# A seven-product MoE kernel: order of the sums' tiles, place of the rounding, operands copied from x

## The chip, the cores and the metric

One core of a Trainium2 chip. The metric is the device time of one execution in microseconds (us). Most executions of a kernel agree within 0.3%.

## The reference, cut to what matters

```python
x = attention(q, k, v)            # k and v averaged over 8 neighbours; 4 batches, 8 heads, 576 tokens, 64 wide
x = x.reshape(2304, 512)          # N tokens, D
p = domain_probs / (domain_probs.sum(-1, keepdims=True) + 1e-09)
for e in range(4):                # moe_w1 [4, 512, 1024], moe_w2 [4, 1024, 512]
    h = np.maximum(x @ w1[e], 0)
    y += p[:, e:e+1] * (h @ w2[e])
a, b = y @ g_w1, y @ g_w2         # [512, 1024] each, float64 inputs
out = (a * b @ g_w3) @ g_wout     # [1024, 1024], [1024, 512]
```

## The kernel before, in words

**Number form.** Each matrix product is made of three matmuls: every operand is held as a high and a low part in fp32r (`hi_lo`, L175: ScalarE, short ACT, copies the high part at L176, another engine subtracts at L177), and `mm3` (L170 to 173) adds high x low, low x high and high x high in one PSUM bank.

**Stages.** A lead of some 25 us brings in q, k, v and makes the first block of x. Then expert 0 runs over 6 blocks of 384 tokens, with 8 units per block (`run_units`; one unit is the hidden rows `expert_h` and, two units later, their second products). Between the halves of the units, `between(n)` runs the pieces of attention for later blocks that lie in the list `hooks[n]`, and the loop after it those in `also[n]`; n counts half units, about 2.1 us each. `accumulate` (L667) multiplies by the weight p at L671 and stores a block of the result `acc_d` at L672.

Experts 1 to 3 run over 4 batches of 576 tokens each (`batch`, L1123), twelve in all. A batch first makes the hidden rows, in 4 calls of `hidden(j)`, each a `seven` (L882): seven products of half-size blocks (Strassen's way in Winograd's form) in place of eight. The operand holds for each half kc of the depth 7 parts in high and low: B11, B21, B22, which are quarters of x itself, and T1 to T4, sums of quarters. VectorE (DVE) adds the products up at L888: `u`, `v`, then the pair `c1` (lower sums), `u` again, then the pair `c0` (upper sums). `c0` and `c1` come from one ring of three tiles, in the order in which they are asked for. `sink` finishes a pair: ReLU on ScalarE at L1114, the high part at L176, the low part on GpSimd (POOL) at L177. The sink of `c1` runs inside its seven, that of `c0` after the first product of the next seven (`settle`). PSUM has eight banks that the products take in turn.

Then come the second products, two half-batches g of 8 steps, 12 matmuls each, into four banks. At the end of a half, VectorE multiplies by p (L1179, four times) and GpSimd adds to `acc` (L1180). In steps 0 to 7, eight DMAs (`fetch_operand`, L792) bring the next batch's operand. In an expert's last batch, `weights_of(j)` (from L718) makes the next expert's seven weight blocks and their sums; the sums `s` (L733 to 736) have one tile for all j. All DMAs are issued on SP's queue in program order.

**The rounding.** The float64 weights of the last stages come as two 32-bit words and are rounded by VectorE and GpSimd in 80 steps (`Rounding.step`, L260): seven or eight operations on VectorE (L271 to L278, for g_w3 a transposition at L309), one on GpSimd (L279), a load (L251), and a store of the step before (L297, L312 four times, or L700). `load` keeps two loads in flight. Before the change a middle batch does 3 steps in its sevens (after seven 1, 2 and 3), 3 in steps 1, 3, 5 of the second products and 2 in steps 9 and 11.

**Operands.** While expert 0's blocks 2 and 3 run, GpSimd adds the parts of x (`keep_x`, L527, in hooks from 35 on) and SP stores the sum to DRAM (`x_d`). From half unit 53 on, `load_x` (L746) loads it batch by batch, `prepare_x` (L827) makes the four sums (L834 to 837) and splits all seven parts, and `keep_operand` stores the whole operand of a batch to DRAM in quarters. Meanwhile `at_pairs` places `weights_of` 0, 1, 2 of expert 1 at units 36, 38, 41.

**w2.** For expert 1 it is split at the end of expert 0. For experts 2 and 3, eight splits lie in the sevens of the expert's first batch, one on VectorE and one on GpSimd per seven.

**The start.** `fetch` issues loads in the order of use when a staging place is free; during the lead only those in `soon`. q tiles from the fourth on come as `qb` in small packets (L447) and are transposed by VectorE (`make_qT`, L462).

Of the kernel before, what the change touches and what calls it, by code (L numbers as in the profile page):

```python
# [17 lines left out]
def fused_kernel(  # L18
# [93 lines left out]
    def packed(base, sizes, most):  # L112
        rings, at = {}, 0
# [25 lines left out]
    p_area = area("p", HT, F32, "pb")  # L139
    ap1, ap2 = area("ap1", 4 * XO, F32, "ap1"), area("ap2", 3328, F32, "ap2")  # L140
    acc_a = Places(acc=row(plain, 0, XT, 2))
    xfpool = Places(xf=row(plain, 2 * XT, HT, 4))
# [92 lines left out]
    class Rounding:  # L235
# [8 lines left out]
        def load(self):  # L244
            while self.todo and len(self.loaded) < 2:
# [74 lines left out]
    with tc.manual_schedule():  # L320
# [9 lines left out]
            **packed(ap2, [("kb", NCH * 2 * D * 4, 1), ("pT", P * 4, 1)], 3328))  # L330
# [194 lines left out]
        x_d = dpool.tile([P, KC, NT], F32, tag="x", name="x")  # L525
# [86 lines left out]
        hooks[3] = kT1[:1]  # L612
        hooks[4] = kT1[1:] + do_qT(TPB + 1)
# [14 lines left out]
        for n, i in enumerate((1, 2, 0, 3, 4, 5)):  # L628
            for hp in range(NP):
                hooks[35 + 4 * n + hp].append((None, lambda i=i, hp=hp: keep_x(i, hp)))  # L630
# [126 lines left out]
        wop_home = [2, 3, 4, 0]  # L757
# [24 lines left out]
        def part_of(b, kc, n):  # L782
            step = 2 * XO // 4 // PIECES
            cols = slice(n * step, (n + 1) * step)
            return whole(kc)[:, cols], kept_x[b][kc].rearrange("p n a s -> p (n a s)")[:, cols]

        def keep_operand(b, kc, ns=range(PIECES)):
            for n in ns:
                here, there = part_of(b, kc, n)
                nc.sync.dma_start(there, here)  # L790

        def fetch_operand(b, kc, n):  # L792
            here, there = part_of(b, kc, n)
            nc.sync.dma_start(here, there)
            xo_next[kc] = x_places[kc]

        def enter_preps():
            late["small"] = Places(xr=Ring(area("x0h", XT, F32, "xr"), [0]), t=Ring(area("x0l", XT, F32, "t"), [0]))
# [555 lines left out]
```

## Time and profile before

| | |
|---|---|
| runs | 1264.73, 1264.85, 1265.68 us (median 1264.85) |
| profiled execution | 1264.25 us |
| its span, first to last instruction | 1262.5 us |
| TensorE matmuls busy | 95% of the span |
| VectorE, GpSimd, ScalarE busy | 69%, 41%, 30% |
| DMA moved | 230.1 MB, mean 182 GB/s |

PE is TensorE (PEld its weight load), DVE is VectorE, ACT is ScalarE, POOL is GpSimd, SPq is SP's queue, which issues the DMAs. L171 is line 171 of the kernel before. "out<-in" names the tiles written and read. PEclk is the granted TensorE clock as a share of full speed, 2.4 GHz; 0.5 is 1.2 GHz. A matmul's busy time overlaps the next one's, so a full PE is not a PE at its peak.

### The profile page before, as it was taken

Reading aid. Unit: us, or ns where it says so; the run is one execution under the profiler, and the core shown is the slowest. Engines: PE = TensorE matmul, PEld = TensorE weight load, DVE = VectorE, ACT = ScalarE, POOL = GpSimd, SP = SyncE. Lnnn points to the kernel's source line nnn. Section 1 sums busy time; section 2 is a strip of 40 time slices with the busy share of each in tenths; the row PEclk is TensorE's granted clock in tenths of the full one; section 3 lists DMA queues with packets and bytes.
Section 4 is the critical chain, followed back from the end, with each engine's and each line's share of the span. In section 5 each row is a group of like instructions: output and inputs, shape, how many; then the busy total and the mean of one; then the engine's idle time right before and its main releaser. Section 6 shows DMA issues by size and latency. Waiting matters only on the chain.

```text
span 1262.5 us, 21704 instructions
## 1 busy us (share of the span) xinstructions
PE 1194.8 (95%) x7965; PEld 1142.5 (90%) x7965; DVE 871.3 (69%) x1855; ACT 373.1 (30%) x687; POOL 516.9 (41%) x569
## 2 busy tenths in 40 slices
PE   7899999989999999789999989999999999999998
PEld 6799999889999989789999979999977999999998
DVE  7677545575777777667677777777759777785554
ACT  4433333344131224313122341220336233241010
POOL 6765441133444346535434654454420222252112
PEclk9899999999999999999999989999999999999999
DMA  8757335786645663564766255656467155665541
GB/s 196 181 135 163 119 105 205 250 293 223 230 165 201 176 207 97 160 195 129 230 193 213 83 176 199 204 198 206 160 191 266 44 203 192 238 232 199 214 175 42
DMA packets 182191, 230.10 MB, mean 182 GB/s; under 512 B 52860, under 2 KB 121540, under 8 KB 182084
## 3 DMA queue, kind: packets, MB, share of 16 engines
q1 hardware_dynamic: 182084, 228.72, 56.6%
q8 instruction: 62, 1.02, 0.3%
q14 instruction: 45, 0.37, 0.1%
HBM read 152.08 MB, written 76.58 MB: 181 GB/s over the span
## 4 chain that ended last, share of the span: by engine, by line
PE 48%; DVE 15%; POOL 12%; DMA 11%; issue 7%; ACT 4%; SPq 2%; POOLq 0%; DVEq 0%; ACTq 0%
PE g L171 9%; PE g L172 9%; PE g L173 9%; POOL round L177 6%; PE s L171 6%; PE s L173 6%; PE s L172 6%; DVE plain L888 4%; ACT plain L1114 2%; POOL x5l L279 2%; POOL plain L1180 2%; DMA w<-x5l 2%; ACT round L176 2%; DMA x5h<-in_moe_w_dram 2%; PE sc L475 1%
## 5 line engine op out<-in xcount | busy, mean ns | idle before, releaser
L177 POOL TENSOR_TENSOR round<-plain,round 128x576 fp32r<-128x576 f32 x128 | 185.9, 1454 | 357.5 <-ACT round L176 301.5
L171 PE MATMUL g<-round,w2h 128*128 128x288 f32 (+1 forms) x960 | 299.3, 312 | 27.6 <-DVE plain L888 20.2
L172 PE MATMUL g<-round,w2l 128*128 128x288 f32 (+1 forms) x960 | 294.1, 306 | 0.0
L173 PE MATMUL g<-round,w2h 128*128 128x288 f32 (+1 forms) x960 | 294.0, 306 | 0.0
L171 PE MATMUL s<-xo,wh 128*128 128x288 f32 x840 | 252.9, 301 | 14.1 <-DVE plain L888 8.5
L173 PE MATMUL s<-xo,wh 128*128 128x288 f32 x840 | 250.7, 298 | 0.0
L172 PE MATMUL s<-xo,wl 128*128 128x288 f32 x840 | 250.4, 298 | 0.0
L171 PEld LDWEIGHTS g<-round,w2h 128*128 128x128 f32 x960 | 183.9, 192 | 34.7 <-DVE plain L888 23.0
L172 PEld LDWEIGHTS g<-round,w2l 128*128 128x128 f32 x960 | 184.0, 192 | 0.0
L173 PEld LDWEIGHTS g<-round,w2h 128*128 128x128 f32 x960 | 183.5, 191 | 0.0
L171 PEld LDWEIGHTS s<-xo,wh 128*128 128x128 f32 x840 | 160.5, 191 | 17.4 <-DVE plain L888 9.5
L888 DVE TENSOR_TENSOR plain<-s,plain 128x288 f32<-128x288 f32 x320 | 133.4, 451 | 42.6 <-PE s L173 25.2
L172 PEld LDWEIGHTS s<-xo,wl 128*128 128x128 f32 x840 | 160.5, 191 | 0.2
L173 PEld LDWEIGHTS s<-xo,wh 128*128 128x128 f32 x840 | 160.6, 191 | 0.0
L176 ACT ACTIVATE round<-plain 128x576 fp32r<-128x576 f32 x132 | 89.7, 682 | 162.0 <-DVE plain L1207 159.0
L279 POOL TENSOR_TENSOR x5l<-x5l 128x256 f32<-128x256 f32 x80 | 58.7, 734 | 180.4 <-DVE x5l L278 180.4
L1114 ACT ACTIVATE plain<-plain 128x576 f32<-128x576 f32 x96 | 65.3, 680 | 218.7 <-DVE plain L888 218.7
L888 DVE TENSOR_TENSOR plain<-s,x5h 128x288 f32<-128x288 f32 x160 | 67.2, 454 | 65.1 <-POOL round L177 54.4
L890 ACT ACTIVATE plain<-s 128x288 f32<-128x288 f32 x80 | 31.7, 396 | 230.8 <-PE s L173 230.8
L171 PE MATMUL g<-xl,round 128*128 128x384 f32 x192 | 67.4, 351 | 4.6 <-DVE round L656 4.6
L656 DVE SCALAR_TENSOR_TENSOR round<-g,round 128x384 fp32r<-128x384 f32 x48 | 26.4, 552 | 61.6 <-ACT round L655 61.5
L173 PE MATMUL g<-xh,round 128*128 128x384 f32 x192 | 65.3, 340 | 0.0
(238 smaller groups left out, 2275.6 us busy)
## 6 DMA issues: line engine op xcount, KB each, us to landing
xo<-keptx SPq DMA_DIRECT2D x72, 504.0 KB
raw<-in_moe_w_dram SPq DMA_DIRECT2D x64, 256.0 KB
x5h<-in_moe_w_dram SPq DMA_DIRECT2D x64, 256.0 KB
keptx<-xo SPq DMA_DIRECT2D x32, 504.0 KB
plain<-acc SPq DMA_DIRECT2D x12, 1152.0 KB
acc<-plain SPq DMA_DIRECT2D x12, 1152.0 KB
kept<-xo SPq DMA_DIRECT2D x12, 576.0 KB
xo<-kept SPq DMA_DIRECT2D x10, 576.0 KB
```

The costliest lines, as they stand in the source:

```text
L171: nc.tensor.matmul(ps, lh, rl, start=first, stop=False)
L172: nc.tensor.matmul(ps, ll, rh, start=False, stop=False)
L173: nc.tensor.matmul(ps, lh, rh, start=False, stop=last)
L176: nc.scalar.activation(hi, src, AF.Copy)
L177: (lo_eng or nc.vector).tensor_tensor(lo, src, hi.bitcast(F32), op=ALU.subtract)
L279: nc.gpsimd.tensor_tensor(a, a, b, op=ALU.add)
L475: nc.tensor.matmul(sc[off:off + n, (hp % 2) * W:(hp % 2 + 1) * W], qT[:, hp, off:off + n], kT_t[b][:, hp * W:(hp + 1) * W], start=True, st ...
L656: nc.vector.scalar_tensor_tensor(hl, ps, 0.0, hh.bitcast(F32), op0=ALU.max, op1=ALU.subtract)
L888: nc.vector.tensor_tensor(to, one, two, op=ALU.add)
L890: nc.scalar.activation(x, product(j, A11, B11), AF.Copy)
L1114: nc.scalar.activation(r, r, AF.Relu)
L1180: nc.gpsimd.tensor_tensor(acc[:, d, cols], acc[:, d, cols], part, op=ALU.add)
```

## The change

1. `seven` asks for `c1` before `c0`, and takes a function `meanwhile` that it calls after the second product's addition.
2. The rounding keeps three loads in flight (three places). A middle batch does one step in its sevens, in seven 2 (an expert's last batch, but not the very last, two, in sevens 1 and 2), and seven in the second products, at steps 1, 3, 5, 7, 9, 10, 12.
3. `acc` and `pb` are loaded after seven 1 instead of ahead of the batch.
4. w2 is streamed in the order of use (`turn_of`). Five of its eight splits move to VectorE, in steps 11 to 15 of the last batch before; three stay in the first batch's sevens, on GpSimd.
5. The operand's B parts are copied by DMA from the high and low parts of x into the DRAM tile `kept_x[b]`. GpSimd adds the parts of x in SBUF for the sums; only the sums are split, and stored by `keep_sums`. The first batch's B parts are fetched back by `fetch_parts`.
6. The batches go 2, 3, 0, 1, then 1, 0, 3, 2, then 2, 3, 0, 1 (before 0 to 3, 3 to 0, 0 to 3). `at_pairs` is 38, 41, 46; blocks of x are freed and reused in another order (`wop_home`).
7. In the lead the second `qb` is in `soon`, and its transposition moves from hook 4 to hook 3.
8. Areas: one `acc` tile in expert 0 instead of two; `ap2` is merged into `p_area`.

```diff
-    acc_a = Places(acc=row(plain, 0, XT, 2))
-    xfpool = Places(xf=row(plain, 2 * XT, HT, 4))
+    acc_a = Places(acc=Ring(plain, [0]))
...
-            while self.todo and len(self.loaded) < 2:
+            while self.todo and len(self.loaded) < 3:
...
-        def keep_x(i, hp):
-            xh, xl = x_t[i]
-            xf = xfpool.tile([P, BLK], F32, tag="xf")
-            nc.gpsimd.tensor_tensor(xf, xh[:, hp].bitcast(F32), xl[:, hp].bitcast(F32), op=ALU.add)
-            nc.sync.dma_start(x_d[:, hp, i * BLK:(i + 1) * BLK], xf)
+        kept_x = [dpool.tile([P, 2, 2, 7, HB], F32, tag=f"keptx{b}", name="keptx") for b in range(B)]
+        def keep_x(i, m):
+            src = x_t[i][m].bitcast(F32)
+            done = 0
+            while done < BLK:
+                b, at = divmod(i * BLK + done, S)
+                a, at = divmod(at, HB)
+                n = min(BLK - done, HB - at)
+                part = src[:, :, done:done + n]
+                if a == 0:
+                    for half in range(2):
+                        nc.sync.dma_start(kept_x[b][:, :, m, half, at:at + n], part[:, 2 * half:2 * half + 2])
+                else:
+                    nc.sync.dma_start(kept_x[b][:, :, m, 2, at:at + n], part[:, 2:])
+                done += n
...
-        hooks[3] = kT1[:1]
-        hooks[4] = kT1[1:] + do_qT(TPB + 1)
+        hooks[3] = kT1[:1] + do_qT(TPB + 1)
+        hooks[4] = kT1[1:]
...
-        wop_home = [2, 3, 4, 0]
+        wop_home = [0, 2, 3, 4]
...
+        def keep_sums(b, kc, ms=range(2)):
+            sums = whole(kc).rearrange("p (n a s) -> p n a s", n=2, s=HB)
+            for m in ms:
+                nc.sync.dma_start(kept_x[b][:, kc, m, 3:], sums[:, m, 3:])
+        def fetch_parts(b, kc):
+            there = whole(kc).rearrange("p (n a s) -> p n a s", n=2, s=HB)
+            for m in range(2):
+                nc.sync.dma_start(there[:, m, :3], kept_x[b][:, kc, m, :3])
+            xo_next[kc] = x_places[kc]
+        def rows_of_x(b, kc):
+            r = late["small"].tile([P, 2, 2, HB], F32, tag="xr")
+            flat = r.rearrange("p n a s -> p n (a s)")
+            done = 0
+            while done < S:
+                i, at = divmod(b * S + done, BLK)
+                n = min(S - done, BLK - at)
+                hi, lo = (t.bitcast(F32).rearrange("p (n k) s -> p k n s", k=2)[:, kc, :, at:at + n] for t in x_t[i])
+                nc.gpsimd.tensor_tensor(flat[:, :, done:done + n], hi, lo, op=ALU.add)
+                done += n
+            sums_t[kc] = None, r
+        def sums_of_x(kc):
+            _, r = sums_t[kc]
+            t = late["small"].tile([P, 4, HB], F32, tag="t")
...
+        def split_sums(kc):
+            (_, th), (_, tl) = x_places[kc]
+            hi_lo(th, tl, sums_t.pop(kc)[0])
...
-        def seven(j, sink):
+        def seven(j, sink, meanwhile=None):
-            c0, c1 = (late["small"].tile([P, 2, HB], F32, tag="c", name=t, bufs=3) for t in ("c0", "c1"))
+            c1, c0 = (late["small"].tile([P, 2, HB], F32, tag="c", name=t, bufs=3) for t in ("c1", "c0"))
...
             add(u, product(j, S2, T2), x)
+            if meanwhile:
+                meanwhile()
             add(v, product(j, S3, T3), u)
...
+        for n, (b, kc) in enumerate((b, kc) for b in order for kc in range(2)):
             begin = 2 * FIRST + 5 * n
+            at_place(begin - 1, lambda b=b, kc=kc: rows_of_x(b, kc))
+            at_place(begin, lambda kc=kc: sums_of_x(kc))
+            at_place(begin + 1, lambda kc=kc: split_sums(kc))
+            for m in range(2) if b != order[-1] else ():
+                at_place(begin + 2 + m, lambda b=b, kc=kc, m=m: keep_sums(b, kc, [m]))
+            if b == order[-1]:
+                at_place(begin, lambda b=b, kc=kc: fetch_parts(b, kc))
+        at_pairs = {38: 0, 41: 1, 46: 2}
...
-        soon = [("qb", TPB)] + [("k", 1, c) for c in range(NCH)]
+        soon = [("qb", TPB)] + [("k", 1, c) for c in range(NCH)] + [("qb", TPB + 1)]
...
-            acc = small.tile([P, KC, S], F32, tag="acc")
-            nc.sync.dma_start(acc, acc_d[:, :, b * S:(b + 1) * S])
-            pb = load_pb(e, b)
             for j in range(NJ):
-                hidden(j)
+                some = j == 2 or last and not end and j == 1
+                hidden(j, (lambda: round_some(1)) if some else None)
...
-                if n == 0 and e > 1:
-                    stream.split(nc.vector)
+                if n == 0 and e > 1 and j < FC - AHEAD:
                     stream.split()
...
-                if j and not (last and j == 3):
-                    round_some(1)
+                if j == 1:
+                    acc = small.tile([P, KC, S], F32, tag="acc")
+                    nc.sync.dma_start(acc, acc_d[:, :, b * S:(b + 1) * S])
+                    pb = load_pb(e, b)
...
                     elif last:
                         if step in (1, 4, 7, 10):
                             weights_of((step - 1) // 3)
+                        if step >= 2 * FC - AHEAD:
+                            stream.split(nc.vector)
...
-                    if step in (1, 3, 5) and (end or not last) or step in (9, 11) and not last:
+                    if step in (1, 3, 5, 7) and (end or not last) or step in (9, 10, 12) and not last:
                         round_some(1)
...
-        orders = {e: list(range(B))[::1 if e % 2 else -1] for e in range(1, E)}
+        orders = {1: [2, 3, 0, 1], 2: [1, 0, 3, 2], 3: [2, 3, 0, 1]}
```

`order` is [0, 1, 3, 2] and AHEAD is 5. `step = g * 8 + k` counts the steps of the second products; `last` is an expert's last batch, `end` the very last.

## Rows read from the trace of the kernel before

**Rows 1.** Page, part 1: engine, busy us (share of the span) xinstructions

```profile
PE 1194.8 (95%) x7965; PEld 1142.5 (90%) x7965; DVE 871.3 (69%) x1855; ACT 373.1 (30%) x687; POOL 516.9 (41%) x569
```

**Rows 2.** Stages: start:end width, PE, PEld, DVE, ACT, POOL busy (x), PEclk, DMA, GB/s

```profile
0.00:50.00 50.00, 37.47 (x217) 31.86 (x218) 34.47 (x59) 19.76 (x40) 34.89 (x67) 0.94 0.77 188
...
192.47:294.33 101.86, 93.55 (x519) 92.59 (x517) 59.44 (x107) 36.25 (x64) 21.74 (x17) 0.97 0.68 233
...
294.33:928.83 634.50, 596.48 (x4322) 587.10 (x4321) 464.18 (x1093) 174.30 (x302) 307.20 (x296) 0.98 0.57 182
```

**Rows 3.** Same view, single stretches: a hidden stage, second products, expert 0

```profile
349.09:371.43 22.34, 22.34 (x170) 22.34 (x169) 16.56 (x42) 8.80 (x16) 11.27 (x11) 1.00 0.52 173
...
529.73:562.47 32.74, 27.68 (x195) 27.08 (x193) 23.47 (x56) 4.70 (x8) 14.63 (x15) 0.95 0.58 168
...
200.00:225.00 25.00, 25.00 (x146) 25.00 (x145) 14.91 (x27) 7.93 (x13) 0.00 (x0) 1.00 0.58 213
```

**Rows 4.** Waits of PE, 294.33 to 928.83: us in total, times, longest us

```profile
PE g L171 <- DVE plain L888: 20.2, 12, 3.8
...
PE s L171 <- DVE plain L888: 8.5, 3, 3.0
...
PE s L171 <- DMA xo<-keptx: 3.3, 4, 1.8
```

**Rows 5.** Groups of DVE, 294.33 to 928.83: busy us, mean ns, idle before <-releaser

```profile
L888 DVE TENSOR_TENSOR plain<-s,x5h 128x288 f32<-128x288 f32 x96 | 39.5, 453 | 56.2 <-POOL round L177 51.6 <-PE s L173 1.8 <-DMA acc<-plain 1.6
...
L1179 DVE TENSOR_TENSOR s<-g,ap 128x288 f32<-128x288 f32 x46 | 20.9, 454 | 26.5 <-POOL plain L1180 26.3 <-PE g L173 0.2
...
L177 DVE TENSOR_TENSOR w2l<-raw,w2h 128x512 fp32r<-128x512 f32 x8 | 12.8, 1598 | 7.7 <-ACT w2h L176 7.7
...
L177 DVE TENSOR_TENSOR round<-raw,round 128x512 fp32r<-128x512 f32 x7 | 4.9, 707 | 5.7 <-ACT round L176 5.7
```

**Rows 6.** Timeline of DVE: start us, us, line, operation [idle before <-releaser]

```profile
375.43 0.82 DVE L888 TENSOR_TENSOR plain<-s,x5h 128x288 f32<-128x288 f32 x2 [1.30 <-POOL round L177]
...
377.66 0.29 DVE L273 TENSOR_SCALAR x5l<-x5l 128x256 f32<-128x256 f32 x1
...
377.99 1.49 DVE L275 TENSOR_SCALAR x5l<-x5l 128x256 uint32<-128x256 uint32 x1
...
437.53 0.29 DVE L271 TENSOR_SCALAR x5l<-x5h 128x256 uint32<-128x256 uint32 x1 [2.54 <-DMA x5h<-in_moe_w_dram]
...
442.14 0.30 DVE L271 TENSOR_SCALAR x5l<-x5h 128x256 uint32<-128x256 uint32 x1 [2.14 <-DMA x5h<-in_moe_w_dram]
...
444.54 0.45 DVE L1179 TENSOR_TENSOR s<-g,ap 128x288 f32<-128x288 f32 x1
```

**Rows 7.** Waits of SP's queue: us in total, times, longest us

```profile
SPq L1127 <- DMA acc<-plain: 53.3, 12, 5.9
```

**Rows 8.** Timeline of DVE, end of the last batch of expert 1

```profile
502.23 1.01 DVE L177 TENSOR_TENSOR wl<-raw,wh 128x512 fp32r<-128x512 f32 x2
```

**Rows 9.** Groups of instructions, whole span, POOL and ACT

```profile
L177 POOL TENSOR_TENSOR round<-plain,round 128x576 fp32r<-128x576 f32 x128 | 185.9, 1454 | 357.5 <-ACT round L176 301.5
...
L1114 ACT ACTIVATE plain<-plain 128x576 f32<-128x576 f32 x96 | 65.3, 680 | 218.7 <-DVE plain L888 218.7
...
L530 POOL TENSOR_TENSOR plain<-xh,xl 128x384 f32<-128x384 f32 x24 | 23.5, 1008 | 6.9 <-DVE xl L177 6.9
```

**Rows 10.** Groups of DVE, 192.47 to 294.33

```profile
L834 DVE TENSOR_TENSOR t<-xr 128x288 f32<-128x288 f32 x8 | 3.6, 453 | 8.4 <-DMA xr<-x 8.4
```

**Rows 11.** Waits of PE, first 50 us, then 192.47 to 294.33

```profile
PE sc L475 <- DVE ap L462: 4.5, 1, 4.5
...
PE g L171 <- DVE round L656: 4.6, 2, 2.9
...
PE g L171 <- DVE plain L671: 3.7, 1, 3.7
```

**Rows 12.** Timeline of SP's queue: start us, us, line, DMA xcount

```profile
36.70 4.36 SPq L447 DMA_DIRECT2D stxl<-in_q_dram  x8
```

More of the change, by code (lines that the diff above doesn't have):

```diff
@@ L110, in row, with packed @@
         return Ring(base, [at + size * n for n in range(bufs)])
-    def packed(base, sizes, most):
-        rings, at = {}, 0
+    def packed(base, sizes, most, begin=0):
+        rings, at = {}, begin
         for tag, size, bufs in sizes:
@@ L627, in fused_kernel @@
             hooks[10 * i + 4][:0] = do_attend(i)
-        for n, i in enumerate((1, 2, 0, 3, 4, 5)):
-            for hp in range(NP):
-                hooks[35 + 4 * n + hp].append((None, lambda i=i, hp=hp: keep_x(i, hp)))
+        for i in range(NB):
+            for m in range(2):
+                hooks[35 + 4 * i + 2 * m].append((None, lambda i=i, m=m: keep_x(i, m)))
         for b, at_v, at_k, at_kT in ((1, 3, None, None), (2, 15, 15, 20), (3, 26, 25, 30)):
@@ L780, in fused_kernel, with fetch_operand @@
         PIECES = 4
-        def part_of(b, kc, n):
+        def fetch_operand(b, kc, n):
             step = 2 * XO // 4 // PIECES
             cols = slice(n * step, (n + 1) * step)
[L785 to L794, printed above, removed]
-            xo_next[kc] = x_places[kc]
+            nc.sync.dma_start(whole(kc)[:, cols], kept_x[b][:, kc].rearrange("p n a s -> p (n a s)")[:, cols])
+            xo_next[kc] = x_places[kc]
@@ new lines, in keep_sums @@
+        def keep_sums(b, kc, ms=range(2)):
[4 more added lines that the diff above has]
+            there = whole(kc).rearrange("p (n a s) -> p n a s", n=2, s=HB)
+            for m in range(2):
+                nc.sync.dma_start(there[:, m, :3], kept_x[b][:, kc, m, :3])
[11 more added lines that the diff above has]
+            sums_t[kc] = None, r
@@ L797, in enter_preps @@
         def enter_preps():
[L798 removed]
+            late["small"] = Places(xr=Ring(plain, [2 * XT]), t=Ring(plain, [XT]))
         def enter_weights():
@@ L936, in rows, with at_place @@
             return w3_blocks[u[1][0]][1] if u[0] == "w" else TPB
-        kept_x = [[dpool.tile([P, 2, 7, HB], F32, tag=f"keptx{b}{kc}", name="keptx") for kc in range(2)] for b in range(B)]
         x_places = []
-        preps = [(b, kc) for b in (1, 2, 3, 0) for kc in range(2)]
+        order = [0, 1, 3, 2]
         FIRST = ATT_BLOCKS * FC + 4
         also = {}
-        for n, (b, kc) in enumerate(preps):
-            begin = 2 * FIRST + 5 * n
-            also.setdefault(begin - 3, []).append(lambda b=b, kc=kc: load_x(x_d, b, kc))
-            for m in range(3):
-                also.setdefault(begin + m, []).append(lambda b=b, kc=kc, m=m: prepare_x(kc, x_places[kc], n=m))
-            for m in range(PIECES if b else 0):
-                also.setdefault(begin + 3 + m, []).append(lambda b=b, kc=kc, m=m: keep_operand(b, kc, [m]))
-        also[2 * FIRST - 3].insert(0, enter_preps)
-        also[2 * FIRST].insert(0, enter_late)
-        at_pairs = {36: 0, 38: 1, 41: 2}
-        also.setdefault(2 * 36, []).append(enter_weights)
+        def at_place(n, f):
+            also.setdefault(n, []).append(f)
+        at_place(2 * FIRST - 1, enter_preps)
+        at_place(2 * FIRST, enter_late)
+        for n, (b, kc) in enumerate((b, kc) for b in order for kc in range(2)):
+            begin = 2 * FIRST + 5 * n
+            at_place(begin - 1, lambda b=b, kc=kc: rows_of_x(b, kc))
[6 more added lines that the diff above has]
+        at_pairs = {38: 0, 41: 1, 46: 2}
+        also.setdefault(2 * 38, []).append(enter_weights)
         for n, j in at_pairs.items():
@@ L1107, in load_pb, with hidden @@
             return pb
-        def hidden(j):
+        def hidden(j, meanwhile=None):
             def sink(n, c, other):
@@ L1115, in sink @@
                 hi_lo(t[:, 0], t[:, 1], r, nc.gpsimd)
-            seven(j, sink)
+            seven(j, sink, meanwhile)
         def round_some(n):
@@ L1146, in batch @@
                     add_pair(e + 1, j)
-                for fc in range(FC):
+                for fc in turn_of:
                     add_w2(e + 1, fc)
```

24 lines of the change are left out of this document (15 added, 9 removed).

## Prediction

> **What bounds the kernel now.** The profiled execution took 1264.25 us, 0.60 under the median of the runs (1264.85); its span is 1262.5, so 1.75 lie around it. The sum below is made on the profiled execution. I read the page's busy times first [rows 1]: TensorE's matmuls fill 95% of the span, VectorE 69%. So only time that TensorE loses can be won, and the shares don't say where it is lost. The busy times by stage do [rows 2], held against undisturbed stretches [rows 3]. A hidden stage is 28 products of 6 matmuls; its 168 (the row counts two neighbours) took 22.34 us, 0.133 each. The twelve batches, 4320 such matmuls (row: 4322), would take 574.5 and take 634.5: **60.0 lost**. The stage 192 to 294 holds 516 matmuls of 384 columns (row: 519); at 25/144 = 0.174 (row: 146, two at the edges) they take 89.6 and took 101.9: **12.3 lost**. The first 50 us have 12.5 idle and a granted clock of 0.94, 3.0 more. The code of what follows 929 is not touched.
>
> Next, who ends TensorE's waits [rows 4]. In the batches it is VectorE's additions at L888, 20.2 + 8.5 = 28.7 in 15 waits; the clock took a good part of the rest. The second-product stretch from 529.73 shows the pair: 5.1 idle, and 0.95 of the clock over 32.7 us, 1.6 more [rows 3].
>
> Why is VectorE late? A seven is 42 matmuls, 5.6 us. VectorE's seven additions take 7 x 0.45 = 3.2 [rows 5]. The third, the first into the tile of the lower sums, waits about 1.3 for GpSimd [rows 6]: 51.6 in all [rows 5]. That tile is the previous seven's upper one, whose rounding ends late. Then comes one rounding step: 2.4 alone (442.14 to 444.54), 3.5 beside GpSimd, when one operation of 0.25 to 0.3 takes 1.49 [rows 6]. 3.2 + 1.3 + 3.5 = 8.0 against 5.6, three times per batch: VectorE ends the sevens some 6 us behind. TensorE can run eight PSUM banks ahead, no further, and so the second products begin with a wait.
>
> **Part by part.**
>
> *Lower sums take their tile first.* With three tiles, the lower sums of seven j now get the tile of the upper sums of j-2, the upper ones that of the lower of j-1. The new pair is 5.6 us apart or more; its chain (two activations of 0.68, GpSimd's 1.45 [rows 9]) takes 2.8. I take the whole wait as gone. If it stayed, a seven without rounding would still be 4.5 against 5.6, so this edit alone decides little.
>
> *Rounding.* A middle batch keeps 8 steps: 1 in a seven (3.2 + 3.5 = 6.7, 1.1 behind, made good in the next), 7 in the second products. The third product of the third seven must be taken when TensorE comes to its bank again, 6.4 us after writing; the step leaves 2.9 spare. In the second products VectorE has 3.5 + 3 x 2.4 = 10.7 of steps in the first half (12.8 long), 3.0 of multiplications (four of 0.45, and 26.5/23 = 1.2 of waits for GpSimd [rows 5]), then 3.3 + 2 x 2.4 = 8.1: 21.8 of the 25.5 us that 192 matmuls take. Loads are the open point: 437.53 to 442.14 a step came every 4.6 us, held 2.1 by its load [rows 6]. Three loads in flight instead of two should bring it near 2.9, since a load then has two steps to land; ends 2.4 and 4.6. On SP's queue each step issues a load and a store (four where it transposes); behind them stand the next operand's eight transfers. Those waited for a late VectorE before and start earlier now.
>
> *acc and pb loads after the second seven.* SP stood 53.3 us in 12 waits before them for the store of the batch before [rows 7]. There now only steps with 10 us to spare stand behind them; acc is first used 24 us later. Cost 0; without that cover a late acc would hold GpSimd's addition.
>
> *w2.* At two changes of expert, eight splits stood in the sevens; four on VectorE took 1.60 each [rows 5]. Now three stay, on GpSimd (3 x 1.45 = 4.4 of 5.6), and five go to VectorE in the last half-batch, behind four weights_of that hang on one tile of sums. The fourth's VectorE part ended at 503.24, 28.2 after the stretch began at 475.05 [rows 8]; about 5 of that was the lag. So 23 + 5 x 1.6 = 31, and the next batch needs the first bank of that half at 25.5 + 3.2 = 28.7: 2.3 wait, 1.6 of clock, **about 4 each**, 0 (0.71 each, as w_out's splits [rows 5]) to 9 (five waits for loads). The slow row is w2l at 1.60 beside GpSimd. The Trainium skill ("SBUF — State Buffer", Who interferes with whom) has a VectorE instruction with two SBUF inputs wait for the whole of a GpSimd one that reads SBUF, which speaks against this move; by it, each behind a whole operation of 1.45, the five would take 5 x (0.71 + 1.45) = 10.8 instead of 8.0, 5.6 us more over both changes.
>
> Batches together, losses left: the first 2 (weights_of stays in its sevens, and the first load of the rounding has nothing ahead of it), two changes 8, four batches of transposed steps 1 each, others about 0.2: 15 of 60.0. **Gain 45**; 25 to 56.
>
> *x.* Before, GpSimd adds x (24 x 1.01 [rows 9]), SP stores it and loads it 16 times. VectorE waited 8.4 for that in this stage [rows 10], SP being behind block stores, and TensorE waited 4.6 + 3.7 for VectorE [rows 11]. After: 36 copies of 98 to 295 KB straight from x in an earlier stretch, the 24 stores of operand quarters here become 12 of 590 KB (and the eight in the first batch four), the first batch's operand is completed by four loads, and GpSimd adds eight times 1152 columns, 8 x 3.0, in a stage where it was busy 21.7 of 102 [rows 2]. It runs ahead by its own semaphores, so no wait; cover gone, up to 3 per operand. VectorE also drops the splits of the B parts. Left: at the second weights_of, now beside the same block's multiplications, about 2 with 1.6 of clock. **Gain 8.5**; 3 to 12.
>
> *Start.* TensorE waited 4.5 at 39.8 for VectorE's transposition of the second q tile [rows 11], whose eight transfers went out at 36.70 [rows 12]. They now go out right behind the first k loads, for the same 4.4 us of SP; behind them stand the last k chunk and w2 loads. Gain 4.5 + 3.0 of clock, less about 1.5: **6**; -1 (they delay the start's loads by their 4.4) to 8.
>
> *At nothing:* order of batches, homes of weights, merged areas, one acc tile instead of two (stores 35 us apart), at_pairs later by 2 to 5 units (the sevens need them later still), the order of w2. If at_pairs came late, the first batch's sevens would wait.
>
> Sum: 45 + 8.5 + 6 = 59.5; 1264.25 - 59.5 = 1204.75, **1205 us**; own range 1193 to 1220.
>
> **Rivals.** (a) *Operands late.* Four steps now share the first half with 4.0 MB of operands. For: TensorE did wait for these (3.3 in four [rows 4]). Against: they start once the sevens have read the old ones, and no longer when a lagging VectorE lets SP go on. Price: nine changes of batch within an expert x (2.0, a little over the longest such wait, + 1.6 of clock) = 32: 1237.
> (b) *Slower: loads set the pace of seven steps.* If steps come 4.6 apart as at 437, VectorE has 0.5 + 7 x 4.6 + 3.0 = 35.7 us before the last multiplications, the first of which frees its bank at 36.2 where TensorE wants it at 28.7; nine batches lose 7.5 + 1.6 = 9.1: 1205 + 82 = 1287. It starts to cost at a step of 3.5 and eats all the gain at 4.3. For: those rows [rows 6]. Against: they are two deep, and the step itself is 2.4.
> (c) *TensorE isn't held by the lag*, only by banks and chains that stay: the batches keep their 60, 1264.25 - 14.5 = 1250. Against: sevens whose VectorE is on time (349.09) lose nothing.
> (d) *It doesn't do what it says*: new waits for GpSimd's additions and SP's copies eat all: 1264.
>
> **Numbers.** Chances: forecast 0.66, (a) 0.15, (b) 0.07, (c) 0.06, (d) 0.06, half of it on either side. Range 1193 to 1238: forecast and (a); left out are (b), (c), (d). A measurement of this kernel can tell 0.2% (2.5 us) from no change. Faster 0.66 + 0.15 + 0.06 + 0.02 = 0.89, same 0.03, slower 0.07 + 0.01 = 0.08.
>
> **What would show it.** L888 no longer waits for GpSimd's rounding; TensorE's waits for L888 fall from 28.7 to under 8; a middle batch takes 48 us; no VectorE wait for xr; no 4.5 at 39.8; and at the two changes of expert a wait of 2 to 4 for L1179. Wrong it is if steps in the second products come over 3.5 apart, if TensorE waits for operands at most batch starts, or if the 192 to 294 stage loses over 8.

## The result, and the profile after

| | before | after |
|---|---|---|
| median of the runs | 1264.79 us (1261.14 to 1265.68) | 1207.81 us (1206.68 to 1208.88) |
| profiled execution, its span | 1264.25, 1262.5 | 1207.31, 1205.6 |

The ratio is 0.9555 (95% interval 0.9534 to 0.9576). In the changed kernel most lines have other numbers: L925 is the sevens' addition (before L888), L1225 the multiplication by p (L1179), L176 the low parts (L177), L270 the first operation of a rounding step (L271), L680 `accumulate`'s multiplication (L671).

On the page after, TensorE is busy for 97% of the span and VectorE for 72% [rows 1]. The busy times by stage answer to [rows 2, 3]: expert 0's tail, the twelve batches, and one middle batch (columns: stretch, its length, busy time and instructions of each engine, granted clock, DMA share, GB/s).

```profile
185.46:279.56 94.10, 91.71 (x518) 91.07 (x517) 51.56 (x91) 28.90 (x48) 36.74 (x26) 0.98 0.49 167
279.56:871.11 591.55, 577.96 (x4322) 575.38 (x4322) 468.42 (x1095) 174.83 (x302) 306.51 (x296) 1.00 0.61 194
575.66:623.43 47.77, 47.77 (x362) 47.77 (x361) 40.77 (x103) 11.89 (x20) 23.66 (x25) 1.00 0.71 209
```

The batches went from 634.50 to 591.55, 42.95 less; the tail from 101.86 to 94.10, 7.8 less; what lies ahead of it from 192.47 to 185.46, 7.0 less. Behind the batches 0.8 came back in the next stage. The sum is the span's 56.9. The second row against the third shows what is left: twelve undisturbed batches would take 573.2, so about 18 us are still lost.

TensorE's waits in the batches after, which answer to [rows 4] (columns: us in total, times, longest):

```profile
PE s L170 <- DVE s L1225: 10.9, 5, 3.0
PE s L170 <- DVE pb L925: 2.7, 2, 1.5
```

Before, TensorE waited 28.7 us for VectorE's additions, mostly ahead of the second products. Now these waits are 2.7, all second products run undisturbed, and what is left stands at the start of the first products, where a bank is held by VectorE's late multiplication.

VectorE's waits in the batches after answer to [rows 5]. L270 is the first operation of a rounding step; `x5h` is where a step's load lands, `x5l` the tile that the step writes, from which its result is stored (here to `gate` or `wo`):

```profile
DVE plain L925 <- ACT plain L927: 22.6, 28, 1.3
...
DVE x5l L270 <- DMA gate<-x5l: 13.1, 9, 3.7
DVE plain L925 <- PE s L172: 10.7, 14, 1.2
DVE x5l L270 <- DMA wo<-x5l: 8.7, 6, 3.7
...
DVE x5l L270 <- DMA x5h<-in_moe_w_dram: 0.9, 2, 0.7
```

The 51.6 us that the additions waited for GpSimd's rounding are gone. So are nearly all waits for the rounding's loads from `in_moe_w_dram`: 0.9 is left of 24.5. Grown are the waits for ScalarE (22.6, before 6.8) and those for the rounding's stores: 13.1 + 8.7 = 21.8, before 12.6. A step writes one of two places (`dtmp`, L845 of the changed kernel) and so waits until the result of the step two before has been stored. Before, the same groups were:

```profile
DVE x5l L271 <- DMA x5h<-in_moe_w_dram: 24.5, 12, 3.3
...
DVE x5l L271 <- DMA gate<-x5l: 7.1, 4, 2.7
...
DVE x5l L271 <- DMA wo<-x5l: 5.5, 2, 2.8
```

### The profile page after: what moved, and what is told of

It reads as the page before. It is cut to its first block, busy times and chain, and to the rows that moved or that the text cites. A ratio compares the mean times of both kernels' runs of the same rounds, so it can differ in the third digit from the quotient of the medians.

```text
span 1205.6 us, 21677 instructions
## 1 busy us (share of the span) xinstructions
PE 1171.2 (97%) x7965; PEld 1125.8 (93%) x7965; DVE 867.4 (72%) x1841; ACT 366.7 (30%) x671; POOL 515.0 (43%) x559
## 4 chain that ended last, share of the span: by engine, by line
PE 68%; DVE 12%; DMA 8%; issue 5%; POOL 4%; ACT 2%; SPq 1%; DVEq 0%; POOLq 0%; ACTq 0%
PE g L170 11%; PE g L171 11%; PE g L172 11%; PE s L170 11%; PE s L171 10%; PE s L172 10%; DMA raw<-in_moe_w_dram 2%; PE x_ps L520 1%; POOL plain L1226 1%; DMA gate<-x5l 1%; DVE plain L925 1%; PE sc L474 1%; DVE x5l L275 1%; DMA raw<-w 1%; PE at_ps L508 1%
## 5 line engine op out<-in xcount | busy, mean ns | idle before, releaser
L176 POOL TENSOR_TENSOR round<-plain,round 128x576 fp32r<-128x576 f32 x128 | 186.6, 1463 | 314.3 <-ACT round L175 290.0
L170 PE MATMUL g<-round,w2h 128*128 128x288 f32 (+1 forms) x960 | 292.7, 305 | 2.4 <-DVE plain L680 2.1
L171 PE MATMUL g<-round,w2l 128*128 128x288 f32 (+1 forms) x960 | 291.1, 303 | 0.0
L172 PE MATMUL g<-round,w2h 128*128 128x288 f32 (+1 forms) x960 | 291.1, 303 | 0.0
L170 PE MATMUL s<-xo,wh 128*128 128x288 f32 x840 | 249.8, 297 | 13.6 <-DVE s L1225 10.9
L172 PE MATMUL s<-xo,wh 128*128 128x288 f32 x840 | 248.6, 296 | 0.0
L170 PEld LDWEIGHTS g<-round,w2h 128*128 128x128 f32 x960 | 180.5, 188 | 3.8 <-DVE plain L680 2.4
L925 DVE TENSOR_TENSOR plain<-s,plain 128x288 f32<-128x288 f32 x320 | 134.0, 452 | 67.0 <-PE s L172 33.8
L171 PEld LDWEIGHTS g<-round,w2l 128*128 128x128 f32 x960 | 180.6, 188 | 0.0
L172 PEld LDWEIGHTS g<-round,w2h 128*128 128x128 f32 x960 | 180.6, 188 | 0.0
L170 PEld LDWEIGHTS s<-xo,wh 128*128 128x128 f32 x840 | 158.4, 189 | 15.9 <-DVE s L1225 12.3
L172 PEld LDWEIGHTS s<-xo,wh 128*128 128x128 f32 x840 | 158.5, 189 | 0.0
L927 ACT ACTIVATE plain<-s 128x288 f32<-128x288 f32 x80 | 31.7, 397 | 238.2 <-PE s L172 238.0
L925 DVE TENSOR_TENSOR plain<-s,pb 128x288 f32<-128x288 f32 x160 | 67.8, 455 | 15.5 <-PE s L172 5.8
```

Source lines behind the costliest of these rows:

```text
L170: nc.tensor.matmul(ps, lh, rl, start=first, stop=False)
L171: nc.tensor.matmul(ps, ll, rh, start=False, stop=False)
L172: nc.tensor.matmul(ps, lh, rh, start=False, stop=last)
L176: (lo_eng or nc.vector).tensor_tensor(lo, src, hi.bitcast(F32), op=ALU.subtract)
L925: nc.vector.tensor_tensor(to, one, two, op=ALU.add)
L927: nc.scalar.activation(x, product(j, A11, B11), AF.Copy)
```

## The experiments

All are variants of the changed kernel unless said otherwise; all ratios are to the kernel before, measured beside them.

**1. The tiles' order undone.**

```diff
-c1, c0 = (late["small"].tile([P, 2, HB], F32, tag="c", name=t, bufs=3) for t in ("c1", "c0"))
+c0, c1 = (late["small"].tile([P, 2, HB], F32, tag="c", name=t, bufs=3) for t in ("c0", "c1"))
```

> The changed kernel with one thing undone: a seven asks for the tile of its upper sums (c0) first again, so that its lower sums take the tile of the previous seven's upper ones. Theory (the place of the rounding steps decides): a seven without a rounding step is then 3.2 + about 1.3 of wait = 4.5 us of VectorE against 5.6 of TensorE, so the wait fits in; only the seven with the step (8.0) ends 2.4 late, and the next makes up 1.1 of it. VectorE's third addition waits for GpSimd again, some 50 us in all, but TensorE loses at most 0.6 per batch: 1208 to 1215 us. Rival (the order of the tiles is the main term of the gain): TensorE's waits for the additions come back by half or more, 15 to 25 us in all: 1223 or more.

Measured: 1244.7 us, ratio 0.9868 (0.9839 to 0.9897). The rival is right, and the time lies well above its 1223: this one line is worth 37 us. TensorE's waits in the batches, of this kernel:

```profile
PE s L170 <- DVE s L1225: 25.7, 11, 3.6
PE s L170 <- DVE pb L925: 10.2, 9, 2.2
```

The additions on VectorE show why. Here is its timeline over a seven without a rounding step, with the first multiplications of the second half in this batch and the next (columns: start, length, operation, idle before it and what ended it):

```profile
387.65 0.45 DVE L1225 TENSOR_TENSOR s<-g,pb 128x288 f32<-128x288 f32 x1
...
394.25 0.46 DVE L925 TENSOR_TENSOR plain<-s,plain 128x288 f32<-128x288 f32 x1 [0.74 <-ACT plain L927]
394.81 0.46 DVE L925 TENSOR_TENSOR pb<-s,plain 128x288 f32<-128x288 f32 x1
397.10 0.82 DVE L925 TENSOR_TENSOR plain<-s,pb 128x288 f32<-128x288 f32 x2 [1.83 <-POOL round L176]
397.84 1.18 DVE L925 TENSOR_TENSOR plain<-s,plain 128x288 f32<-128x288 f32 x3
399.75 0.46 DVE L925 TENSOR_TENSOR plain<-s,plain 128x288 f32<-128x288 f32 x1 [0.74 <-ACT plain L927]
...
437.45 0.45 DVE L1225 TENSOR_TENSOR s<-g,pb 128x288 f32<-128x288 f32 x1
```

And the same places in the changed kernel:

```profile
380.27 0.45 DVE L1225 TENSOR_TENSOR s<-g,pb 128x288 f32<-128x288 f32 x1
...
383.11 0.45 DVE L925 TENSOR_TENSOR plain<-s,plain 128x288 f32<-128x288 f32 x1
383.67 0.46 DVE L925 TENSOR_TENSOR pb<-s,plain 128x288 f32<-128x288 f32 x1
384.23 0.82 DVE L925 TENSOR_TENSOR plain<-s,pb 128x288 f32<-128x288 f32 x2
384.97 1.18 DVE L925 TENSOR_TENSOR plain<-s,plain 128x288 f32<-128x288 f32 x3
386.88 0.46 DVE L925 TENSOR_TENSOR plain<-s,plain 128x288 f32<-128x288 f32 x1 [0.73 <-ACT plain L927]
...
426.65 0.45 DVE L1225 TENSOR_TENSOR s<-g,pb 128x288 f32<-128x288 f32 x1
```

A VectorE that lags takes 399.75 - 394.25 = 5.50 us for a seven in the old order, and 386.88 - 383.11 = 3.77 in the new one. TensorE takes 5.6. In the old order a lag is never made up; in the new one each seven gives back 1.8. Two waits are in the 5.50: 1.83 for GpSimd, and 0.74 for ScalarE's copy of the seven's first product (L927), which stands on ScalarE behind the two operations, 0.69 each, on the lower sums of the seven before. The 2.9 left is the seven additions, a little under 7 x 0.45 since they overlap. Over the whole batch, from one multiplication to the same one a batch later, VectorE takes 437.45 - 387.65 = 49.8 in the old order and 426.65 - 380.27 = 46.4 in the new; TensorE's undisturbed batch of 47.8 lies between the two. This pair is near the low end in both kernels. Without the two periods in which the next expert's weights are made, the nine others take 51.5 in the mean in the old order (49.2 to 55.2) and 48.2 in the new (46.4 to 50.6). That is 3.3 apart, and the batches as a whole differ by 37.1, or 3.1 each. In the old order VectorE's additions waited only 5.5 us in all for TensorE, so these periods are VectorE's own pace.

**2. The rounding's place undone.**

```diff
-hidden(j, (lambda: round_some(1)) if some else None)
+hidden(j)
...
+if j and not (last and j == 3):
+    round_some(1)
...
-if step in (1, 3, 5, 7) and (end or not last) or step in (9, 10, 12) and not last:
+if step in (1, 3, 5) and (end or not last) or step in (9, 11) and not last:
```

> The changed kernel with one thing undone: the rounding steps stand where they stood before (in a middle batch one after each of sevens 1, 2 and 3, then steps 1, 3, 5, 9, 11 of the second products). Theory (the place of the rounding steps decides): three sevens of 6.7 us of VectorE against 5.6 leave it 3.3 behind at the second products, against some 6 in the kernel before; TensorE waits for the additions there again, 1 to 3 us in each of nine middle batches with the clock that follows: 1217 to 1235 us; the waits at the starts of the sevens (13.6 now) fall below 5. Rival (the order of the tiles is the main term): with the tiles' order kept VectorE is late by little that the PSUM banks don't cover: 1213 or less.

Measured: 1200.25 us, ratio 0.9511 (0.9489 to 0.9533): faster than the changed kernel, 7.6 by the medians, 5.6 by the ratios. It lies within the rival's bound, but that this part of the change is a loss neither of the two had said. TensorE's waits in the batches of this kernel:

```profile
PE s L170 <- DVE s L1226: 5.1, 2, 3.1
PE g L170 <- DVE plain L925: 3.0, 3, 1.6
```

The middle batches lose nothing; the two waits of 5.1 in all and two of the three others stand at the changes of expert. VectorE's waits in its additions show that it is on time now:

```profile
DVE plain L925 <- PE s L172: 20.9, 48, 1.2
...
DVE plain L925 <- ACT plain L927: 5.0, 6, 1.3
```

It waits 20.9 us in 48 short waits for TensorE's products (10.7 in the changed kernel) and only 5.0 for ScalarE (22.6), a wait that shows where it lags. A step in a seven fills time in which VectorE would wait for TensorE anyway, and with the steps spread so, VectorE's waits for their stores are 14.5 (8.4 + 6.1) where the changed kernel has 21.8.

**3. The splits of w2 undone.**

```diff
-AHEAD = 5
+AHEAD = 0
...
-if n == 0 and e > 1 and j < FC - AHEAD:
+if n == 0 and e > 1:
+    stream.split(nc.vector)
     stream.split()
```

> The changed kernel with one thing undone: the eight splits of w2 for experts 2 and 3 stand in the sevens of the expert's first batch again, one on VectorE and one on GpSimd per seven. Theory (the five splits at the end of a chain of four weights_of hold the multiplications, as predicted): the losses at the two changes of expert, 4.8 and 2.7 us now, fall below 1 each; the first batches lose up to 3 each instead, in sevens that hold a split of 1.0 to 1.6 and GpSimd's: 1203 to 1209 us. Rival (the four weights_of hold them, and the splits only stand behind): the losses at the changes stay above 2 each, and the first batches' come on top: 1210 to 1216.

Measured: 1212.07 us, ratio 0.9607 (0.9588 to 0.9625). Two stretches of this kernel, the first batch of expert 2 and the first products of the second (columns as above):

```profile
476.59:525.71 49.12, 48.64 (x363) 47.91 (x362) 38.22 (x81) 15.99 (x28) 29.23 (x27) 1.00 0.65 208
525.71:554.60 28.89, 24.07 (x170) 23.83 (x169) 23.00 (x61) 9.58 (x17) 14.09 (x14) 0.94 0.53 153
```

The theory has the mechanism and not the price. The changes themselves lose 0.2 and 0.1 at their first products, down from 4.8 and 2.7. But the first batch takes 49.1, and VectorE carries its lag through it: the next first products take 28.9 where 22.3 is undisturbed (29.4 behind the first batch of expert 3). The five splits are rightly placed; the work comes out one batch later when it is put there.

**4. All edits to VectorE's work in the batches undone** (the order, the rounding's place, two loads in flight, w2, and `acc` and `pb` ahead of the batch; the diffs of 1 to 3 and 7 together).

> The changed kernel with all edits to the batches' VectorE work undone together: the tiles' order, the place of the rounding, two loads in flight, the splits of w2, and acc and pb loaded ahead of the batch. What stays of the change is x by DMA, the start, the homes of the weights and the order of the batches. Theory (these edits are the batches' gain of 43, and the rest is the 7.0 before and 7.8 after 185 us): 1245 to 1254 us, with some 28 us of TensorE's waits for the additions. Rival (part of the batches' gain comes from the operands, the areas or the order of the batches): 1235 or less; other rival (the gain before the batches depends on these edits too): over 1257.

Measured: 1245.11 us, ratio 0.9867 (0.9848 to 0.9886), at the theory's lower end. The batches take 630.0 against 634.5 before: 4.5 of the 43 come from operands, areas or the order of the batches, the rest from these edits. Experiment 1, which undoes the order alone, took 1244.7: with the old order, the four other edits together are worth nothing that can be measured.

**5. The tiles' order alone, in the kernel before** (the diff of 1, reversed).

> The kernel before with one edit of the change alone: a seven asks for the tile of its lower sums (c1) first. Theory (a new one, from the run with this edit undone: VectorE's time per batch, its waits in the sevens included, is what TensorE is held to; with the old order a lagging seven takes VectorE 5.5 us and can't catch up on TensorE's 5.6, with the new one 3.8): the old place of the rounding, two loads in flight and the old splits of w2 stand, yet the middle batches lose next to nothing; about 7 at each of two changes of expert and 2 or 3 in the first batch stay of the batches' 60: a gain of 38 to 48, 1216 to 1227 us. Rival (the prediction's step: this edit alone decides little, the gain needs the others beside it): 1245 us or more.

Measured: 1232.22 us, ratio 0.9754 (0.9736 to 0.9771): a gain of 31 us by the medians, 33.4 by the spans, and 33.5 in the batches, which take 601.0. That is less than the theory's 38, and far above the rival's. The middle batches of expert 3 lose nothing with the rounding at its old place, but in the batches with transposed steps, with two loads in flight, 1.5 to 3 are still lost.

**6. More work on VectorE.** Does the old order cost through GpSimd's lateness or through VectorE's time?

```diff
-add(v, product(j, S3, T3), u)
+p3 = product(j, S3, T3)
+for _ in range(3):
+    add(v, p3, u)
```

> The changed kernel with VectorE's third product addition in each seven done three times over into the same tile (the same result; two additions of 0.37 to 0.45 us more per seven, where the wait for GpSimd stood in the old order). Theory (VectorE's time per batch decides, whatever it is spent on): 3.0 to 3.6 us more per batch on an engine that needs 46 to 47 of TensorE's 47.8: 12 batches lose some 20 to 35 us more: 1227 to 1243 us. Rival (the old order cost by its dependency through GpSimd, which delays the finished hidden rows, and VectorE had room): 1206 to 1213 us.

Measured: 1258.8 us, ratio 0.9966 (0.9952 to 0.9981): 51 more, and 44.9 of it in the batches (636.40 against 591.55). The timeline at the places shown above:

```profile
387.13 0.45 DVE L1227 TENSOR_TENSOR s<-g,pb 128x288 f32<-128x288 f32 x1
...
389.97 0.45 DVE L925 TENSOR_TENSOR plain<-s,plain 128x288 f32<-128x288 f32 x1
390.52 1.44 DVE L925 TENSOR_TENSOR pb<-s,plain 128x288 f32<-128x288 f32 x3
...
394.71 0.46 DVE L925 TENSOR_TENSOR plain<-s,plain 128x288 f32<-128x288 f32 x1 [0.73 <-ACT plain L927]
...
437.43 0.45 DVE L1227 TENSOR_TENSOR s<-g,pb 128x288 f32<-128x288 f32 x1
```

The three additions take 1.44 where one took 0.46, so each seven costs 0.98 more (4.74 instead of 3.77), 48 sevens 47 us. Of these, 44.9 came out. Behind the batches, where the last stages have sevens too, 8.0 more are lost (342.5 against 334.5); what lies ahead is 1.7 shorter. The batch on VectorE takes 437.43 - 387.13 = 50.3; the nine periods named in experiment 1 take 51.9 in the mean, 3.7 over the changed kernel's, and a batch lost 3.7. This settles it: no wait for GpSimd stands in these sevens, and the loss is as large. VectorE's time per batch is what counts; the changed kernel has practically none to spare. The theory was right in kind and too low: it had taken the 1.4 us between 46.4 and 47.8 as room in every batch, two additions at 0.74 to 0.90 where they took 0.98, and left out the last stages.

**7. Two loads of the rounding in flight.**

```diff
-while self.todo and len(self.loaded) < 3:
+while self.todo and len(self.loaded) < 2:
```

> The changed kernel with two loads of the rounding in flight instead of three. Theory of the prediction (with two, a step in the second products is held to 4.6 us by its load, and the third brings it near 2.9): seven steps end up to 10 late, every middle batch loses 3 to 8 us more: 1235 to 1280 us. Rival (the loads are held by what stands ahead of them on SP's queue and in the DMA queues, the next operand's 4 MB, not by their depth): 1207 to 1216 us.

Measured: 1226.21 us, ratio 0.9708 (0.9689 to 0.9727), between the two. The starts of three steps in the second products of this kernel:

```profile
402.86 0.29 DVE L270 TENSOR_SCALAR x5l<-x5h 128x256 uint32<-128x256 uint32 x1
...
409.46 0.30 DVE L270 TENSOR_SCALAR x5l<-x5h 128x256 uint32<-128x256 uint32 x1 [3.58 <-DMA x5h<-in_moe_w_dram]
...
414.46 0.29 DVE L270 TENSOR_SCALAR x5l<-x5h 128x256 uint32<-128x256 uint32 x1 [2.52 <-DMA x5h<-in_moe_w_dram]
```

and of two of them in the changed kernel:

```profile
405.89 0.28 DVE L270 TENSOR_SCALAR x5l<-x5h 128x256 uint32<-128x256 uint32 x1
...
408.82 0.29 DVE L270 TENSOR_SCALAR x5l<-x5h 128x256 uint32<-128x256 uint32 x1
```

With two loads a step comes 5.0 to 6.6 after the one before, where the prediction had 4.6; with three it comes 2.9 after, the prediction's figure. In the batches VectorE's waits for the loads from `in_moe_w_dram` are 26.3 us here and 0.9 in the changed kernel. But mostly the transposed steps are held so (they issue four stores each, not one; that this is the reason was not tried alone): the four first products behind them take 30.2, 30.6, 27.2 and 28.8 us (24.1, 22.5, 22.3 and 23.7 with three loads), the others together no longer than before. So the whole is 18 us.

**8. Two loads, and the rounding at its old place** (the diffs of 2 and 7).

> The changed kernel with two edits undone together: the rounding steps in their old places, and two loads in flight. With the steps in the second products, the third load was worth 18 us. Theory (that worth comes of steps that follow one another without pause; with three of eight steps 5.6 us apart in the sevens a load has the time it needs, and only the stretches with three steps in a row wait): VectorE's waits for loads cost 0 to 1 us per batch: 1200 to 1209 us. Rival (the third load pays wherever the steps stand, since VectorE's time is short in every batch): 1212 to 1220 us.

Measured: 1205.57 us, ratio 0.9554 (0.9528 to 0.9580), as the theory has it. At the old place the third load is worth 5 us, at the new one 18: it mostly pays for the move.

**9. The start undone.**

```diff
-soon = [("qb", TPB)] + [("k", 1, c) for c in range(NCH)] + [("qb", TPB + 1)]
+soon = [("qb", TPB)] + [("k", 1, c) for c in range(NCH)]
...
-hooks[3] = kT1[:1] + do_qT(TPB + 1)
-hooks[4] = kT1[1:]
+hooks[3] = kT1[:1]
+hooks[4] = kT1[1:] + do_qT(TPB + 1)
```

> The changed kernel with the start undone: the second q tile's loads go out as before, not in the lead, and its transposition stands in hook 4. Theory (the 7.0 us won before 185 us are the wait of 4.5 at 39.8 and the clock behind it): the wait of about 4.5 near 39 us comes back and the time is 1212 to 1216 us. Rival (they come from the smaller x part, the areas or the GpSimd work that went): 1206 to 1210 us.

Measured: 1213.7 us, ratio 0.9611 (0.9594 to 0.9627), 5.9 more than the changed kernel, as the theory has it. TensorE's wait in its first 50 us answers to [rows 11]:

```profile
PE sc L474 <- DVE ap L461: 4.9, 1, 4.9
```

In the changed kernel this wait is 0.4.

**10 to 12. Towards a better version.** All three start from the kernel of 2. In 10 the weights of the next expert are loaded after seven 1 of an expert's last batch (the block in the first cut moves into the loop of the sevens). 11 is 10 with four splits of w2 on VectorE, not five. 12 is 10 with the fourth `weights_of` put behind seven 0 of the next batch (its weights are then loaded behind those of the five splits) and expert 1's second at unit 43.

```diff
-elif last:
+if j == 1 and last and not end:
     for j in range(NJ):
         add_pair(e + 1, j)
     for fc in turn_of:
         add_w2(e + 1, fc)
     stream.fill()
...
-AHEAD = 5
+AHEAD = 4
...
-if n == 0 and e == 1 and j == 0:
+if n == 0 and j == 0:
     weights_of(NJ - 1)
...
-if step in (1, 4, 7, 10):
+if step in (1, 4, 7):
...
-at_pairs = {38: 0, 41: 1, 46: 2}
+at_pairs = {38: 0, 43: 1, 46: 2}
```

> The changed kernel with the rounding steps back in their old places (1200.25 us), and the loads of the next expert's weights issued after seven 1 of an expert's last batch instead of after its sevens. With the old places, what the batches still lose is at the changes of expert: 4.8 and 2.3 us at the first products, 1.3 and 1.9 in the second products that follow. Theory (the chain there, four weights_of and five splits of w2 on VectorE, counts from its first load, for which VectorE waits 2.8): it starts 2 to 3 us earlier, and with the lag the loss behind it shrinks too: 1193 to 1198 us. Rival (the chain is held further on, by GpSimd's share of the splits and by the loads of w2 behind the staging places): 1199 to 1202 us.

> The same as the run with the earlier loads, with four splits of w2 on VectorE at the end of an expert's last batch instead of five; the fourth of the other splits goes to GpSimd in seven 3 of the next batch. Theory (VectorE's chain at the change sets the loss): 1.0 to 1.6 us less at each of two changes where a loss is left: 1190 to 1197 us, 0 to 3 below the run beside it. Rival (GpSimd has no room in those sevens, two halves of 1.45, a rounding part of 0.74 and a split of 1.45 in 5.6 us, and makes the second products late): as the run beside it or up to 4 slower.

> The run with the earlier loads (1198.53 us) and two more edits, both to take VectorE's work out of the way where it ends late: the fourth weights_of of a change of expert goes from step 10 of the last batch to a place behind seven 0 of the next expert's first batch (as expert 1 has it), and expert 1's second weights_of, in expert 0, from unit 41, where the multiplications of block 4 stand behind it, to unit 43. Theory (VectorE's time in the stretch that ends late is all that holds TensorE there): the chain at the change loses the fourth weights_of's 4 us and TensorE's waits of 3.3 and about 2 there go; the first batches that take it over lose up to 1 more; the wait of 2.1 for L680 near 248 us goes, with about 1 of clock: 1188 to 1194 us. Rival (the stretches beside are as full, and the work comes out again where it is put): 1196 to 1202 us.

Measured: 1198.53 us, ratio 0.9502 (0.9478 to 0.9527); 1199.5, ratio 0.9509 (0.9481 to 0.9538); 1200.64, ratio 0.9512 (0.9491 to 0.9534). They can't be told from one another, nor from 2. The time of 10 lies between its theory's range and its rival's; the waits speak for the rival: the first wait for the load fell from 2.8 to 1.5, and TensorE's waits at the changes stayed (5.2, in 2 5.1). In 11 and 12 work was taken from one full stretch and mostly came out in the next: in 11 the first products at the changes lose 5.3 less, and the second products there and the first products behind them 4 more. TensorE's waits of 12, from the page of its whole execution:

```profile
PE g L170 <- DVE plain L925: 4.9, 3, 2.3
...
PE g L170 <- DVE round L665: 3.6, 1, 3.6
PE s L170 <- DVE plain L925: 3.5, 2, 1.9
```

No wait for the multiplication is left in the batches, and none for L680; but the sevens that took the fourth `weights_of` now make TensorE wait 4.9 + 3.5 (5.1 + 3.0 in the batches of 2), and in place of the 2.1 stands a wait of 3.6 near 278 us, behind the third `weights_of`, where the changed kernel had 0.3. The best version is 2, with or without 10: 1199 to 1200 us.

## Why the prediction was right, and where it was not

**The sum.** Forecast 1205, measured 1207.81: the forecast case came true. By terms: batches 45 forecast, 42.95 found; x 8.5 and 7.8; start 6 and 7.0; nothing behind the batches, where 0.8 came back.

**The failed step: "If it stayed, a seven without rounding would still be 4.5 against 5.6, so this edit alone decides little."** Experiment 1 shows 5.50, and with experiment 5 that the edit decides most of the batches' gain: 37 us when it is undone, 33.5 of 42.95 when it stands alone. The 1.3 was read behind a seven with a rounding step [rows 6]; between two sevens without one the wait is 1.83, in the kernel before too:

```profile
360.40 0.82 DVE L888 TENSOR_TENSOR plain<-s,x5h 128x288 f32<-128x288 f32 x2 [1.83 <-POOL round L177]
```

And 0.74 for ScalarE comes on top, which the step left out. 4.5 leaves room to catch up, 5.5 does not.

**The second failed step** is the reason given for the rounding: that the steps in the sevens make VectorE end them late, so that moving them is a gain. With the new order VectorE catches up 1.8 in a seven without a step, and steps at the old place lose nothing (experiment 2). Moved, seven of them stand in the second products, close enough that a step waits for the store of the one two before. The total came out right because the whole change does take VectorE's lag away; the prediction put that down to the wrong edit. That 45 met 42.95 is in part luck: the order gave more than the forecast allowed it, and the move of the rounding cost 7.6 where it was to gain.

**A third step that failed: loads as "the open point" of the rounding.** The third load did what was forecast: the waits for loads fell from 24.5 us to 0.9. But the prediction has no term for a step's wait for the store of the step two before; these waits, 12.6 us before, are 21.8 after. Rival (b)'s point at which the pace begins to cost, 3.5, fits (steps of 5.0 and more cost, steps of 2.9 don't). Its price fits less: with two loads, four first products lose 6.9 each, where it had 9.1 in nine. With three loads some steps are held all the same. The starts of four of the seven steps in the second products of expert 3's first batch, in the changed kernel:

```profile
705.44 0.29 DVE L270 TENSOR_SCALAR x5l<-x5h 128x256 uint32<-128x256 uint32 x1
...
709.33 0.29 DVE L270 TENSOR_SCALAR x5l<-x5h 128x256 uint32<-128x256 uint32 x1 [1.05 <-DMA gate<-x5l]
...
714.52 0.30 DVE L270 TENSOR_SCALAR x5l<-x5h 128x256 uint32<-128x256 uint32 x1 [2.92 <-DMA gate<-x5l]
...
726.00 0.38 DVE L270 TENSOR_SCALAR x5l<-x5h 128x256 uint32<-128x256 uint32 x1 [0.58 <-DMA gate<-x5l]
```

and on SP's queue:

```profile
709.21 0.42 SPq L709 DMA_DIRECT2D gate<-x5l  x1
709.68 1.01 SPq L794 DMA_DIRECT2D xo<-keptx  x2
...
723.51 0.73 SPq L709 DMA_DIRECT2D gate<-x5l  x1
```

The first three come 3.9 and 5.2 us apart, over the 3.5 from which it was to cost, and the next first products wait 2.28 for L1225. The store issued at 709.21, with two transfers of the next operand behind it, holds a step until 714.52; the one issued at 723.51, with none there, holds one until 726.00: 5.3 and 2.5 us. Whether the transfers are the reason was not tried, nor was a third place for the step's result. Nine batch starts apart from the changes lose 10.6 together, where the forecast had 4 for the transposed ones and about 1 for the others; the first batch loses nothing, where it had 2. With 7.5 at the changes that is 18.1 left, for a forecast of 15.

**The changes of expert**: 4 each forecast, 4.8 and 2.7 found, by another sum. VectorE's timeline at the first of them, after:

```profile
474.39 4.15 DVE L176 TENSOR_TENSOR w2l<-raw,w2h 128x512 fp32r<-128x512 f32 x4 [0.47 <-ACT w2h L175]
480.42 0.69 DVE L176 TENSOR_TENSOR w2l<-raw,w2h 128x512 fp32r<-128x512 f32 x1 [1.87 <-ACT w2h L175]
```

The five splits take 4.8, not 8.0, and waits of 0.5 and 1.9 for the high part (whose load is late) make up for some of it. Taken singly in the trace, the first two, beside GpSimd's split of the sums (473.62 to 476.79), take 1.80 and 1.22, the other three, with GpSimd idle, 0.68 or 0.69. Four of them at the old place, in the sevens of experiment 3, take 1.56 in the mean. The Trainium skill's rule ("SBUF — State Buffer", Who interferes with whom), that such a VectorE operation waits for GpSimd's, agrees with these durations; the 10.8 worked out from it was wrong since only two of the five met a GpSimd operation.

**The other signs.** The additions wait no longer for GpSimd's rounding; TensorE's waits for them fell to 2.7 (under 8 forecast); the best middle batch takes 47.8 (48); no load of x is waited for, though VectorE waits 6.0 us in three for GpSimd's sums of x, where "no wait" was forecast, at no cost to TensorE; the 4.5 at 39.8 is 0.4; TensorE waited for no operand, so rival (a) fell. The stage up to the batches still loses about 4.5 (94.1 against 89.6), 2.1 of it at L680 beside the second `weights_of`, as forecast. Not tried alone: the x part, whose 7.8 is read from the stage's length only, the loads of `acc` and `pb`, and the order of the batches.

## What to carry to other kernels

Take a helper engine's whole period, its waits included, and hold it against the bound engine's: a mean of 48.2 against 47.8 loses little, one of 51.5 loses what lies above, and what it waits for inside is as dear as its work. Read the cost of a wait from a place where the engine already lags, and see which wait it is: here loads stopped being waited for, and the stores took their place. And test the edits one by one: here one swapped line made more than half of the gain, and the edit beside it that seemed the main one cost 7.6 us.

## What was not expected of the hardware

One VectorE instruction, a w2 split of 128x512, took 1.60 in the mean at its old place and 0.68 to 1.80 at its new one, by what GpSimd did meanwhile: 0.68 with GpSimd idle. The duration of a moved operation has to be taken from a row of the place that it moves to. Beyond that nothing of the hardware came unexpected; the surprises were in the schedule.
